# Another order for a planned kernel of attention, a rational MLP and a top-1 mixture of experts: new priority tables, some planner costs, the expert's choice marked as exclusive with GpSimd

## The chip, the cores and the metric

The kernel runs on one core of a Trainium2 chip. A core has a matrix engine (TensorE; PE in the profile, with its weight loads as PEld), a vector engine (VectorE, DVE), a scalar engine (ScalarE, ACT), a general engine (GpSimd, POOL) and a queue engine (SyncE, SP) that here issues the transfers. Each runs its own list of instructions in order and waits on semaphores for the others. The metric is the device time of one execution in microseconds (us); lower is better.

## What is computed

Three stages in a row, each on the output of the one before, all in fp32 accuracy:

```python
# attention: 4 batches, 8 heads, 1152 keys of 64; queries are averaged in pairs (576 a batch)
q_pool = q.reshape(B, H, S // 2, 2, D).mean(axis=3)
attn = softmax(q_pool @ k.transpose(0, 1, 3, 2) / sqrt(D))
x = (attn @ v).transpose(0, 2, 1, 3).reshape(2304, 512)
# MLP with a rational activation, 512 -> 2048 -> 512
h = x @ w_in
g = (a[0] + a[1]*h + a[2]*h**2 + a[3]*h**3) / (1 + abs(b[0])*abs(h) + abs(b[1])*h**2 + 1e-6)
x = g @ w_out
# mixture of 8 experts, one per token, 512 -> 1024 -> 512
e_idx = argmax(x @ w_gate, axis=1)
for e in range(8):
    mask = e_idx == e
    out[mask] = gate_w[mask] * sigmoid(x @ w_ogate)[mask, e] * (relu(x[mask] @ w1[e]) @ w2[e])
```

## The kernel before

**Numbers.** Every fp32 operand of a large product is split into a high and a low half-precision part (16 bits each), and a product is three matmuls: high by high, high by low, low by high. The splitting is elementwise work for DVE, ACT and POOL, and it is most of what these do.

**Attention** is cut into 144 units (`unit`, lines 894 to 1006): a tile of 128 queries of one head against all 1152 keys. A unit has two score products on PE (lines 925; 1024 keys into the PSUM tile `sab`, the last 128 into a small bank), the row maximum on DVE (the score reduction, line 935, over 1024 keys; line 938 for the rest), a one-column bias on DVE or ACT (lines 945 and 947), the exponentials on ACT (line 953), the split of the probabilities (the rounding copy `ph`, lines 962 and 964, and the residual `pl`, line 968: POOL or DVE), a transposing transfer by SP, and the product with v on PE (line 977). Before a batch, k, v and q are loaded, scaled and split; the scales are worked out in chains of tiny DVE operations (line 730), which write `small`.

**The MLP** is cut into 18 tiles of 128 tokens with four groups of 512 hidden columns each, 72 in all (`group`, lines 1257 to 1345): four first-layer blocks on PE (lines 1276 to 1278), some ten elementwise operations (lines 1287 to 1330: DVE's fused steps at line 1287, the numerator's products at line 1291 and fused steps at line 1315 on POOL or DVE, abs, logarithm and exponential on ACT), the split of the result, and the second-layer matmuls (lines 1338 to 1340). One buffer, `tw`, is shared by all groups. The last DVE row of a group at line 1287 reads `scr` and `hps` and writes `scr`.

**Routing** (`route`, lines 1397 to 1470): behind a tile's fourth group its output is evacuated with a scale (`yr`, line 1443, ACT or DVE), transposed on PE (line 1446), multiplied with the gates (line 1409); then comes the choice, a chain of four tiny DVE operations (`choose`, line 730; the last writes `oh`, 128x8), the ranks on PE (lines 1418 and 1419: by `tri` and by ones), the gate weights, and an indirect transfer by POOL (line 1465) that scatters the tokens to an array in DRAM sorted by expert (`ysort`).

**Experts.** After tile 9 the planned part picks the expert with most tokens so far, and loads and splits its weights; after tile 15 a row at line 1540 reads that expert's count, SP pads its rows, and five slots of 128 sorted rows each are worked (`first_slots`, first layer at lines 1609 to 1611, second at 1625 to 1627) while tiles 16 and 17 end. Then a table of the other slots is made and the rest runs in slots with a fixed order, which the planner doesn't touch.

**What sets the order.** Every operation of the planned part is handed to `plan.add` with a key (about the number of the unit beside which it is due), the engines that may do it with a cost each, what it reads and writes, and whether it is exclusive. `order` (lines 444 to 527) is a list scheduler: again and again it places, over all engines, the operation that can start first by its own account of times; equal starts go by key. To the key is added an entry of `SHIFT` for the operation's kind (name, engines, and a suffix: "." for keys under 9, ":" under 24, "!" from 128, none between), and for an operation that several engines may do, an entry of `BIAS` for kind and engine is added to the start. Exclusive (`port`) means that the planner doesn't place the operation on DVE or POOL while it believes the other of the two to be in another exclusive one; operations that may go to several engines are exclusive if nothing else is said. `plan.trace` then writes each engine's instructions in the order found. So the tables and costs set two things only: which engine does an operation, and where it stands in that engine's list.

```python
if ops[i][8] and e in other:
    s = max(s, port[other[e]])
```

Of the kernel before, what the change touches and what calls it, by code (L numbers as in the profile page):

```python
# [21 lines left out]
SHIFT = {'X/PE': -203.5,  # L22
 'X/PE!': -61.3,
 'X/PE.': 56.9,
 'X/PE:': -56,
 'bias/DVE+ACT': -115.7,
 'bias/DVE+ACT!': 88.3,
 'bias/DVE+ACT.': -79.5,
 'bias/DVE+ACT:': 1.9,
 'chain cf/DVE': 397.7,  # L30
 'chain cf/DVE.': -13.6,
 'chain den/DVE': 102,
 'chain den/DVE!': 66.3,
 'chain den/DVE.': -3.2,
 'chain esc/DVE': 181.5,
 'chain esc/DVE!': 33.5,
 'chain esc/DVE:': 86.2,
 'chain ps/DVE': 9.5,
 'chain ps/DVE!': -176.9,
 'chain ps/DVE:': 17.4,  # L40
 'chain qsc/DVE': -94,
 'chain qsc/DVE.': -4.7,
 'chain qsc/DVE:': -143.1,
 'chain ro/DVE': -47,
 'chain ro/DVE!': 78.8,
 'chain ro/DVE:': 0.2,
 'chain rt/DVE': -0.1,
 'chain rt/DVE!': 21.5,
 'chain rt/DVE:': 1.3,
 'chain sc/DVE': -76.9,  # L50
 'chain sc/DVE.': -188.4,
 'chain wsi/DVE.': 9.2,
 'chain wso/DVE.': -74.1,
 'chain xm/DVE': 15.3,
 'chain xm/DVE.': -1,
 'chain xs/DVE': 284.9,
 'chain xt/DVE': -4.1,
# [48 lines left out]
 'nBl/DVE+POOL.': 6,
 'nrm/DVE+ACT+POOL': 352.5,
 'nrm/DVE+ACT+POOL.': -4.5,
 'nrm/DVE+ACT.': -8.4,
 'nrmQ/DVE+ACT': 835.2,  # L110
 'nrmQ/DVE+ACT:': -0.2,
 'nrmQ/DVE:': -71.1,
 'nrmQl/DVE+POOL': -0.8,
 'nrmQl/DVE+POOL.': -15.4,
 'nrml/DVE+POOL': -3.4,
 'nrml/DVE+POOL.': 57.1,
 'oacc/POOL+DVE': -278.6,
 'oacc/POOL+DVE!': 4.6,
 'oacc/POOL+DVE:': -6.8,
 'p/ACT': 366.4,  # L120
 'p/ACT!': -10.2,
 'p/ACT.': 272.1,
 'p/ACT:': 120.4,
 'p/DVE.': -24,
 'pad/SP.': 10.6,
 'padded/SP!': -19,
 'pads/SP': 173.4,
 'pc/ACT': -66.9,
 'pc/ACT!': -102.5,
 'pc/ACT.': 1.3,  # L130
 'pc/ACT:': 0.8,
 'ph/DVE+ACT+POOL': 4.9,
 'ph/DVE+ACT+POOL!': 5.8,
 'ph/DVE+ACT+POOL.': -21.1,
 'ph/DVE+ACT+POOL:': -2.9,
 'ph/DVE:': 4.3,
 'pl/POOL+DVE': -790.8,
 'pl/POOL+DVE!': 41.7,
 'pl/POOL+DVE.': 7.4,
 'pl/POOL+DVE:': -76.9,  # L140
 'pt/SP': -17.5,
 'pt/SP!': 4.5,
 'pt/SP.': -3.8,
 'pt/SP:': 3,
 'pv/PE': -149.5,
 'pv/PE!': -47.1,
 'pv/PE.': 27.7,
 'pv/PE:': 4.4,
 'qT/SP': 42.7,
 'qT/SP.': 0.7,  # L150
 'qT/SP:': -35.1,
 'qm/DVE': 460.9,
 'qm/DVE.': 1.1,
 'qm/DVE:': 1.4,
 'qr/SP': 72.3,
 'qr/SP.': 170.6,
 'qr/SP:': -5.2,
 'qs/DVE+POOL': 19.6,
 'qs/DVE+POOL.': 107.8,
 'raw/SP.': -1.3,  # L160
 'rawz/SP!': 29.3,
 're/ACT': 188,
 're/ACT!': -29.6,
 're/ACT:': -103.1,
 'rs/ACT': 151.9,
 'rs/ACT!': -59.9,
 'rs/ACT:': -15.8,
 'run/DVE': 0.9,
 'run/DVE!': -22.7,
 'sab/PE': 16,  # L170
 'sab/PE!': 156.4,
 'sab/PE.': 20.1,
 'sab/PE:': -5.3,
 'scr/DVE.': 250.6,
 'sq/ACT.': -4.8,
 'sq/DVE:': -35.2,
 'sum/PE': 10.9,
# [382 lines left out]
def tile_attn_moe_moe2(  # L560
# [139 lines left out]
    xhf = acut(DM, F32, ["xhf0", "xhf1"])  # L700
# [1255 lines left out]
```

## Time and profile before

| what | value |
|---|---|
| times of three runs | 1224.31, 1235.28, 1235.61 us |
| median | 1235.28 us |
| the profiled execution, its own time | 1225.93 us |
| its span | 1224.2 us |
| its granted TensorE clock, mean | 0.937 |
| DVE busy | 971.0 us, 79% of the span |
| PE busy | 975.9 us, 80% |
| ACT busy | 800.7 us, 65% |
| POOL busy | 610.1 us, 50% |

The profile is of one execution, taken by the hardware profiler. Busy is the time in which an engine ran an instruction; a share over the whole span mixes stretches with different limits, so the stretches are read apart. Durations of rows include what an instruction waits inside its own execution. A row of the timeline has its start and length in us, the engine, the line, the operation, what it writes and reads with shapes, and in square brackets the idle time of the engine just before it with what ended that.

### The profile page before, as it was taken

How to read it: one execution, taken by the hardware profiler on the slowest of the kernel's cores; microseconds unless marked ns; L12 is line 12 of the kernel's file. 1: busy time of each engine (PE TensorE's matmuls, PEld its weight loads, DVE VectorE, ACT ScalarE, POOL GpSimd, SP SyncE). 2: the span in 40 equal slices, each digit the busy share in tenths (PEclk: the TensorE clock that was granted, in tenths of full speed). 3: DMA queues.
4: the chain of work that ended last, by engine and by line, in shares of the span. 5: the costliest groups of instructions: out<-in, count | busy, mean ns of one | idle time of the engine just before them, and what ended most of it. 6: DMA issues, size and time to landing. Idle time of an engine off the chain costs nothing. (4 is left out here: it accounts for less than half of the span.)

```text
span 1224.2 us, 30760 instructions
## 1 busy us (share of the span) xinstructions
PE 975.9 (80%) x12213; PEld 687.7 (56%) x12213; DVE 971.0 (79%) x2122; ACT 800.7 (65%) x1174; POOL 610.1 (50%) x421
## 2 busy tenths in 40 slices
PE   0245558878787798889898989898988799899986
PEld 0022345556554566656666765575656577577763
DVE  6998777798999898999998899989897864333354
ACT  1664749789786899799799868885775541122213
POOL 0023358657486786476587756766876530000000
PEclk9997569989899899999999999999999899999998
DMA  8889559989789989989989986798564502333351
GB/s 330 253 184 246 98 125 202 153 148 200 169 151 190 203 159 182 192 165 161 189 150 174 167 173 142 143 195 136 106 117 111 147 27 54 90 79 79 76 177 29
DMA packets 493058, 185.78 MB, mean 152 GB/s; under 512 B 454164, under 2 KB 472596, under 8 KB 492821
## 3 DMA queue, kind: packets, MB, share of 16 engines
q1 hardware_dynamic: 489933, 174.16, 70.9%
q0 software_dynamic: 2960, 9.46, 2.3%
q8 instruction: 99, 1.62, 0.5%
q14 instruction: 66, 0.54, 0.1%
HBM read 60.36 MB, written 11.82 MB: 59 GB/s over the span
## 5 line engine op out<-in xcount | busy, mean ns | idle before, releaser
L968 POOL TENSOR_TENSOR att<-att 128x1152 f16<-128x1152 f32 x91 | 221.8, 2439 | 187.3 <-ACT att L962 165.6
L1276 PE MATMUL hps<-scr,winh 128*128 128x128 f16 x1152 | 218.2, 227 | 25.9 <-DVE scr L1287 21.6
L1277 PE MATMUL hps<-scr,winh 128*128 128x128 f16 x1152 | 218.4, 227 | 0.0
L1278 PE MATMUL hps<-scr,winl 128*128 128x128 f16 x1152 | 218.3, 227 | 0.0
L977 PE MATMUL shared<-att 128*128 128x65 f16 (+3 forms) x4320 | 155.5, 201 | 59.4 <-DMA att<-att 41.6
L935 DVE TENSOR_REDUCE small<-sab 128x1 f32<-128x1024 f32 x144 | 175.0, 1216 | 23.5 <-PE sab L925 16.0
L977 PEld LDWEIGHTS <-att 128*128 128x128 f16 (+1 forms) x4320 | 144.3, 106 | 86.6 <-DMA att<-att 54.5
L953 ACT ACTIVATE att<-sab,small 128x1024 f32<-128x1024 f32 x144 | 172.8, 1200 | 18.4 <-DVE small L730 8.1
L1291 POOL TENSOR_TENSOR scr<-scr 128x512 f16<-128x512 f32 (+1 forms) x96 | 122.6, 1279 | 79.6 <-ACT scr L1330 33.5
L925 PE MATMUL sab<-att 128*128 128x512 f16 x512 | 145.1, 411 | 21.6 <-ACT att L953 13.4
L925 PEld LDWEIGHTS <-att 128*128 128x128 f16 x768 | 73.2, 103 | 122.9 <-issue 72.4
L1277 PEld LDWEIGHTS <-winh 128*128 128x128 f16 x1152 | 117.4, 102 | 43.5 <-issue 33.7
L1276 PEld LDWEIGHTS <-winh 128*128 128x128 f16 x1152 | 118.4, 103 | 16.4 <-issue 3.7
L1278 PEld LDWEIGHTS <-winl 128*128 128x128 f16 x1152 | 117.7, 102 | 0.0
L1287 DVE SCALAR_TENSOR_TENSOR scr<-scr,small,hps 128x512 f32<-128x512 f32 x144 | 106.5, 740 | 13.6 <-ACT hps L1326 7.2
L1609 PE MATMUL sab<-att 128*128 128x128 f16 x608 | 107.8, 223 | 7.6 <-DMA att<-att 5.2
L1338 PE MATMUL yps<-wouth,scr 128*128 128x512 f16 x288 | 109.9, 382 | 3.3 <-DVE small L730 2.3
L1340 PE MATMUL yps<-wouth,scr 128*128 128x512 f16 x288 | 110.1, 382 | 0.9 <-POOL scr L1291 0.9
L1339 PE MATMUL yps<-woutl,scr 128*128 128x512 f16 x288 | 110.1, 382 | 0.0
L1611 PE MATMUL sab<-att 128*128 128x128 f16 x608 | 107.7, 223 | 2.1 <-DVEq L1859 1.5
L1610 PE MATMUL sab<-att 128*128 128x128 f16 x608 | 107.8, 223 | 0.0
L962 ACT CAST att<-att 128x1152 f16<-128x1152 f32 x90 | 103.7, 1153 | 5.0 <-DMA att<-att 4.1
(226 smaller groups left out, 2351.8 us busy)
## 6 DMA issues: line engine op xcount, KB each, us to landing
att<-in_k_dram SPq DMA_DIRECT2D x16, 576.0 KB, 5.6
att<-in_q_dram SPq DMA_DIRECT2D x16, 512.0 KB, 4.6
att<-in_moe_w_dram SPq DMA_DIRECT2D x4, 2048.0 KB, 9.1
att<-in_v_dram SPq DMA_DIRECT2D x14, 576.0 KB, 4.6
woutl<-in_moe_w_out_dram SPq DMA_DIRECT2D x12, 512.0 KB, 7.6
att<-ysort SPq DMA_DIRECT2D x19, 257.0 KB, 3.0
att<-att SPq DMA_TRANSPOSE x137, 5.0
wouth<-in_moe_w_in_dram SPq DMA_DIRECT2D x4, 512.0 KB, 11.2
```

Of the source, the lines that this page charges most:

```text
L925: T.matmul(dst[:, d0:d0 + w], qT[:, H * x + 2 * i + t, :], rhs, start=(x == 0), stop=(x == 1))
L935: A(key - ahead - .6, {"DVE": 1.13}, lambda e: V.reduce_max(mm[:, 0, bi:bi + 1], ab, axis=AX.X), r=[f"sab{par}"] + mt, w=[f"mab{n}"] + ([f ...
L953: return lambda e: S.activation(dst, src, AF.Exp, bias=mm[:, 2, bi:bi + 1], scale=esc[:, 0, i:i + 1])
L968: lambda e: eng(e).tensor_tensor(out=phs[pb][:, 1], in0=p32, in1=ph(), op=SUB),
L977: T.matmul(pvb[p0:p0 + w, bi, 0:d], pt[:, lhs, p0:p0 + w], rhs[:, h, c, :], start=(c == 0 and lhs == 0 and rhs is vh), stop=(lhs == 2 * KC ...
L1276: T.matmul(hp, wh, xh[:, kc, :], start=(kc == 0), stop=False)
L1277: T.matmul(hp, wh, xl[:, kc, :], start=False, stop=False)
L1278: T.matmul(hp, wl, xh[:, kc, :], start=False, stop=(kc == KD - 1))
L1291: return lambda e: eng(e).tensor_tensor(out=out_, in0=i0, in1=i1, op=op)
L1338: T.matmul(yps, a, wouth[:, ff, :], start=(ff == 0), stop=False)
L1339: T.matmul(yps, a, woutl[:, ff, :], start=False, stop=False)
L1340: T.matmul(yps, b_, wouth[:, ff, :], start=False, stop=(ff == KF - 1))
```

## The change

The two tables are written anew with other numbers (237 and 136 entries before, 233 and 145 now), five of the planner's cost literals are set to measured lengths, and the choice of the expert is marked as exclusive. No operation is added, taken out or computed otherwise.

```diff
-SHIFT = {'X/PE': -203.5,
+SHIFT = {'X/PE': -189.5,
- 'pl/POOL+DVE': -790.8,
+ 'pl/POOL+DVE': -1071.9,
...
-BIAS = {('bias/DVE+ACT', 'ACT'): 63.85,
+BIAS = {('bias/DVE+ACT', 'DVE'): -0.87,
- ('ph/DVE+ACT+POOL', 'POOL'): 39.78,
+ ('ph/DVE+ACT+POOL', 'POOL'): 204.46,
...
-        A(key - ahead - 1.2, {"PE": 0.86 * f2}, smm(ab, [(0, 512), (512, 512)]), r=ins, w=[f"sab{par}"])
+        A(key - ahead - 1.2, {"PE": 0.9 * f2}, smm(ab, [(0, 512), (512, 512)]), r=ins, w=[f"sab{par}"])
...
-            A(key + .05 * jj, {"PE": 0.67}, g1(jj), r=[f"xT{s}"] + cols, w=[ht])
+            A(key + .05 * jj, {"PE": 0.7}, g1(jj), r=[f"xT{s}"] + cols, w=[ht])
...
-        LP = {"POOL": 0.68, "ACT": 0.62, "DVE": 0.33}
+        LP = {"POOL": 0.68, "ACT": 0.7, "DVE": 0.45}
...
-        A(k2 + .05, {"POOL": 1.9, "DVE": 0.65}, next_, r=[f"tq{tb}", c], w=[f"tp{tb}"])
+        A(k2 + .05, {"POOL": 2.0, "DVE": 0.65}, next_, r=[f"tq{tb}", c], w=[f"tp{tb}"])
...
-        A(key, {"ACT": 0.57, "DVE": 0.6},
+        A(key, {"ACT": 0.57, "DVE": 0.67},
           lambda e: S.activation(yr[:, 0:DM], yps, AF.Copy, scale=cf("iy")) if e == "ACT" else
...
-        chain(key + .08, choose, r=["y"], w=[f"rt{o}"])
+        chain(key + .08, choose, r=["y"], w=[f"rt{o}"], port=1)
```

The tables are five lines longer, so line 717 of the kernel before is line 722 of the changed one, and so on. What the tables do is seen in the order of the instructions. Three places follow; in all of them a row is line, operation, what it writes and reads, and the shape.

**DVE, the last score reduction of attention.** `sab` is the PSUM tile of the scores, `hps` that of an MLP group's first layer. Before, from row 1557 of DVE's list:

```order
L935 TENSOR_REDUCE small<-sab_75 128x1
L730 CAST small<-small 128x1
L1287 SCALAR_TENSOR_TENSOR scr<-scr,small,hps_77 128x512
L730 SCALAR_TENSOR_TENSOR small<-shared,small 128x4
L947 TENSOR_SCALAR small<-small 128x1
L730 RECIPROCAL small<-small 128x4
L1006 TENSOR_TENSOR att<-shared,small 128x256
L730 RECIPROCAL yr<-small 128x1
L748 SCALAR_TENSOR_TENSOR att<-att,small 128x1024 x2
L1315 SCALAR_TENSOR_TENSOR scr<-scr,small 128x512
L1291 TENSOR_TENSOR scr<-scr 128x512
L1287 SCALAR_TENSOR_TENSOR hps_77<-scr,small,hps_77 128x512
```

In the changed kernel the same reduction is row 1487:

```order
L940 TENSOR_REDUCE small<-sab_75 128x1
L735 TENSOR_SCALAR oh_89<-small 128x8
L1320 SCALAR_TENSOR_TENSOR scr<-scr,small 128x512
L735 SCALAR_TENSOR_TENSOR small<-shared,small 128x4
L735 SCALAR_TENSOR_TENSOR small<-yps,oh_89 128x8 x2
L735 RECIPROCAL small<-small 128x4
L735 CAST small<-small 128x1
L1292 SCALAR_TENSOR_TENSOR scr<-scr,small,hps_78 128x512
L1011 TENSOR_TENSOR att<-shared,small 128x256
L1292 SCALAR_TENSOR_TENSOR hps_78<-scr,small,hps_78 128x512
L943 TENSOR_SCALAR small<-shared,small 128x128
L1292 SCALAR_TENSOR_TENSOR scr<-scr,hps_78 128x512
```

The reduction moved 70 rows forward. Three more of the 72 MLP groups then end behind it.

**DVE, the first read of sorted rows.** Line 717 (now 722) takes the maximum of the first rows fetched from the sorted array; `att` is the storage that they lie in, and the rows at line 1287 (now 1292) are MLP steps. Before, from row 1623:

```order
L1287 SCALAR_TENSOR_TENSOR scr<-scr,hps_78 128x512
L717 TENSOR_REDUCE small<-att 128x1
L1555 TENSOR_SCALAR small<-small 128x1
L1556 TENSOR_SCALAR small<-small 128x1
L1557 TENSOR_SCALAR small<-small 128x1
L1287 SCALAR_TENSOR_TENSOR scr<-scr,small,hps_77 128x512
L717 TENSOR_REDUCE small<-att 128x1
L748 SCALAR_TENSOR_TENSOR att<-att,small 128x512
L1555 TENSOR_SCALAR small<-small 128x1
L1556 TENSOR_SCALAR small<-small 128x1
L1557 TENSOR_SCALAR small<-small 128x1
L1287 SCALAR_TENSOR_TENSOR scr<-scr,small,hps_77 128x512
```

Here the read stands right behind the last step of a group, and row 1639, five rows behind this piece, is tile 16's evacuation (line 1443). In the changed kernel:

```order
L1292 SCALAR_TENSOR_TENSOR hps_78<-scr,small,hps_78 128x512
L1292 SCALAR_TENSOR_TENSOR scr<-scr,hps_78 128x512
L1307 TENSOR_SCALAR scr<-scr,small 128x512
L1296 TENSOR_TENSOR scr<-scr 128x512
L1292 SCALAR_TENSOR_TENSOR scr<-scr,small,hps_77 128x512
L1320 SCALAR_TENSOR_TENSOR scr<-scr,small 128x512
L722 TENSOR_REDUCE small<-att 128x1
L1560 TENSOR_SCALAR small<-small 128x1
L1561 TENSOR_SCALAR small<-small 128x1
L1562 TENSOR_SCALAR small<-small 128x1
L1292 SCALAR_TENSOR_TENSOR scr<-scr,small,hps_77 128x512
L1623 TENSOR_SCALAR small<-att,small 128x1
```

Four MLP rows (lines 1307, 1296, 1292, 1320) now stand between that last step and the read, and tile 16's evacuation isn't in DVE's list: ACT does it, as it does those of tiles 15 and 17.

**PE, the ranks of the last tile.** They are the two products by `tri` and by ones; `sab` is here the output of an expert's first layer (line 1609 to 1611), and `shared` that of its second. Before:

```order
L1610 LDWEIGHTS att
L1610 MATMUL sab_74<-att 128x128
L1611 LDWEIGHTS att
L1611 MATMUL sab_74<-att 128x128
L1418 LDWEIGHTS tri
L1418 MATMUL yps<-oh_89,tri 128x8
L1419 LDWEIGHTS ones_82
L1419 MATMUL yps<-oh_90,ones_82 128x8
L1609 LDWEIGHTS att
L1609 MATMUL sab_75<-att 128x128
L1610 LDWEIGHTS att
L1610 MATMUL sab_75<-att 128x128
```

In the changed kernel:

```order
L1632 LDWEIGHTS att
L1632 MATMUL shared<-att 128x512
L1633 LDWEIGHTS att
L1633 MATMUL shared<-att 128x512
L1634 LDWEIGHTS att
L1634 MATMUL shared<-att 128x512
L1423 LDWEIGHTS tri
L1423 MATMUL yps<-oh_89,tri 128x8
L1424 LDWEIGHTS ones_82
L1424 MATMUL yps<-oh_90,ones_82 128x8
L1614 LDWEIGHTS att
L1614 MATMUL sab_74<-att 128x128
```

The ranks now stand within the first layer of another slot, one earlier, with more of the first slots' blocks behind them: 20 of the first layer and 31 of the second, where 17 and 24 stood.

## Rows read from the trace of the kernel before

**Rows 1.** The page's parts 1 and 2: busy time of each engine; DVE in 40 slices.

```profile
PE 975.9 (80%) x12213; PEld 687.7 (56%) x12213; DVE 971.0 (79%) x2122; ACT 800.7 (65%) x1174; POOL 610.1 (50%) x421
DVE  6998777798999898999998899989897864333354
```

**Rows 2.** Windows: stretch, length, busy PE PEld DVE ACT POOL, clock, DMA share, GB/s.

```profile
92.00:214.00 122.00, 73.98 (x906) 49.74 (x906) 97.80 (x180) 82.06 (x112) 63.32 (x39) 0.72 0.82 168
214.00:857.00 643.00, 555.05 (x7567) 393.76 (x7566) 588.75 (x1362) 534.90 (x801) 425.79 (x272) 0.95 0.91 169
914.50:951.60 37.10, 30.78 (x376) 23.99 (x374) 29.71 (x55) 21.47 (x38) 23.14 (x20) 0.91 0.49 116
951.60:1046.00 94.40, 85.44 (x897) 61.82 (x896) 56.20 (x148) 34.36 (x58) 27.99 (x27) 0.96 0.26 73
1046.00:1224.20 178.20, 157.43 (x1704) 112.02 (x1703) 67.17 (x127) 42.72 (x51) 16.88 (x18) 0.97 0.34 87
```

**Rows 3.** Timeline of DVE, 914 to 1023 us, single rows.

```profile
914.54 1.23 DVE L935 TENSOR_REDUCE small<-sab 128x1 f32<-128x1024 f32 x1 [0.56 <-PE sab L925]
...
922.67 0.68 DVE L1287 SCALAR_TENSOR_TENSOR scr<-scr,hps 128x512 f32<-128x512 f32 x1
...
946.93 0.16 DVE L730 TENSOR_REDUCE small<-yps 128x1 f32<-128x8 f32 x1
...
951.62 0.16 DVE L1540 SCALAR_TENSOR_TENSOR small<-small 128x8 f32<-128x8 f32 x1
...
963.87 0.69 DVE L1287 SCALAR_TENSOR_TENSOR scr<-scr,hps 128x512 f32<-128x512 f32 x1
...
986.77 0.17 DVE L730 TENSOR_REDUCE small<-yps 128x1 f32<-128x8 f32 x1 [2.11 <-PE yps L1409]
```

**Rows 4.** Timeline of DVE and PE at the first read of sorted rows.

```profile
969.90 0.69 DVE L717 TENSOR_REDUCE small<-att 128x1 f32<-128x512 f32 x1 [5.34 <-DMA att<-ysort]
...
976.45 1.12 PE L1446 MATMUL yps<-ident,yr 128*128 128x128 f32 x4 [6.40 <-DVE yr L1443]
```

**Rows 5.** Timeline of PE, 1046 to 1063 us, the rows with a wait.

```profile
1046.58 0.38 PE L1627 MATMUL shared<-att 128*128 128x512 f16 x1 [0.78 <-ACT att L1639]
...
1054.15 0.23 PE L1609 MATMUL sab<-att 128*128 128x128 f16 x1 [2.24 <-DVE small L1557]
...
1062.35 0.22 PE L1609 MATMUL sab<-att 128*128 128x128 f16 x1 [2.67 <-DMA att<-att]
```

**Rows 6.** Tiny chains: timeline at 605 us, then line 730's forms (min/median/max ns), one group's mean.

```profile
604.98 2.36 DVE L730 TENSOR_SCALAR oh<-small 128x8 bf16<-128x8 f32 x1
...
604.94 2.37 POOL L968 TENSOR_TENSOR att<-att 128x1152 f16<-128x1152 f32 x1
...
L730 DVE TENSOR_SCALAR oh<-small x18: 217/404/2364, 233.7 to 1022.9; 128x8 bf16<-128x8 f32 x18
...
L730 DVE SCALAR_TENSOR_TENSOR small<-small x54: 137/212/2406, 44.2 to 1024.3; 128x1 f32<-128x1 f32 x18, 128x2 f32<-128x2 f32 x16, 128x8 f32<-128x8 f32 x16, 128x4 f32<-128x4 f32 x4
...
L730 DVE SCALAR_TENSOR_TENSOR small<-small 128x8 f32<-128x8 f32 x16 | 9.6, 616 | 0.0
```

**Rows 7.** Instructions by line and form: busy us, mean ns, idle before, releaser.

```profile
L730 DVE TENSOR_SCALAR oh<-small 128x8 bf16<-128x8 f32 x18 | 13.6, 753 | 0.2
L947 DVE TENSOR_SCALAR small<-small 128x1 f32<-128x1 f32 x115 | 23.7, 206 | 0.7
L968 DVE TENSOR_TENSOR att<-att 128x1152 f16<-128x1152 f32 x9 | 14.3, 1594 | 0.0
L968 DVE TENSOR_TENSOR scr<-att,scr 128x1152 f16<-128x1152 f32 x7 | 9.6, 1374 | 0.2 <-ACT scr L962 0.2
L1291 DVE TENSOR_TENSOR scr<-scr 128x512 f32<-128x512 f32 x41 | 30.4, 744 | 0.7 <-ACT scr L1300 0.7
L1315 DVE SCALAR_TENSOR_TENSOR scr<-scr,small 128x512 f32<-128x512 f32 x33 | 28.9, 878 | 0.1
L968 POOL TENSOR_TENSOR att<-att 128x1152 f16<-128x1152 f32 x91 | 221.8, 2439 | 187.3 <-ACT att L962 165.6 <-issue 14.2 <-DVE att L964 3.4
```

More of the change, by code (lines that the diff above doesn't have):

```diff
@@ L360 @@
- ('wih/ACT+DVE.', 'DVE'): 66.77,
- ('wil/POOL+DVE.', 'POOL'): 62.66,
- ('woh/ACT+DVE.', 'ACT'): -0.68,
- ('woh/ACT+DVE.', 'DVE'): 9.87,
- ('wol/POOL+DVE.', 'POOL'): 3.57,
+ ('pl/POOL+DVE!', 'POOL'): -1,
+ ('pl/POOL+DVE.', 'DVE'): 88.35,
+ ('pl/POOL+DVE.', 'POOL'): 2.03,
+ ('pl/POOL+DVE:', 'DVE'): 88.28,
+ ('pl/POOL+DVE:', 'POOL'): -0.16,
+ ('qs/DVE+POOL', 'DVE'): 0.04,
+ ('qs/DVE+POOL', 'POOL'): 32.87,
+ ('qs/DVE+POOL.', 'DVE'): 59.25,
+ ('qs/DVE+POOL.', 'POOL'): -1,
+ ('qs/DVE+POOL:', 'DVE'): 0.79,
@@ new lines @@
+ ('tp/POOL+ACT+DVE', 'POOL'): 1.04,
+ ('tp/POOL+ACT+DVE!', 'ACT'): 15.57,
+ ('tp/POOL+ACT+DVE!', 'DVE'): 0.12,
+ ('tp/POOL+ACT+DVE!', 'POOL'): 0.32,
+ ('tp/POOL+ACT+DVE:', 'ACT'): 9.89,
+ ('tp/POOL+ACT+DVE:', 'DVE'): 52.34,
+ ('tp/POOL+ACT+DVE:', 'POOL'): 9.81,
+ ('tp/POOL+DVE!', 'DVE'): -0.32,
+ ('tp/POOL+DVE!', 'POOL'): 69.52,
+ ('tp/POOL+DVE:', 'DVE'): -0.11,
+ ('tq/ACT+DVE!', 'ACT'): 0.24,
+ ('tq/ACT+DVE!', 'DVE'): 14.61,
+ ('tq/ACT+DVE:', 'ACT'): 88.21,
+ ('tq/ACT+DVE:', 'DVE'): -1,
+ ('tw/POOL+ACT+DVE', 'ACT'): 0.41,
@@ new lines @@
+ ('tw/POOL+ACT+DVE', 'DVE'): 0.55,
+ ('tw/POOL+ACT+DVE', 'POOL'): 76.1,
+ ('tw/POOL+ACT+DVE!', 'ACT'): 0.06,
+ ('tw/POOL+ACT+DVE!', 'DVE'): 0.94,
+ ('tw/POOL+ACT+DVE!', 'POOL'): 16.2,
+ ('tw/POOL+ACT+DVE:', 'ACT'): -0.99,
+ ('tw/POOL+ACT+DVE:', 'DVE'): 8.01,
+ ('tw/POOL+ACT+DVE:', 'POOL'): -0.12,
+ ('vh/DVE+ACT+POOL', 'ACT'): -1,
+ ('vh/DVE+ACT+POOL', 'DVE'): 18.82,
+ ('vh/DVE+ACT+POOL.', 'DVE'): 16.5,
+ ('vh/DVE+ACT+POOL.', 'POOL'): 36.44,
+ ('vl/DVE+POOL', 'DVE'): -1,
+ ('vl/DVE+POOL', 'POOL'): 3,
@@ L370 @@
+ ('xh/DVE+ACT+POOL!', 'ACT'): -1,
+ ('xh/DVE+ACT+POOL!', 'DVE'): 7.97,
+ ('xh/DVE+ACT+POOL!', 'POOL'): -1,
  ('xh/DVE+ACT+POOL.', 'ACT'): -1,
[L371 to L381 removed]
@@ L382 @@
[L382 to L394 removed]
+ ('xh/DVE+ACT+POOL.', 'DVE'): 4.14,
+ ('xh/DVE+ACT+POOL.', 'POOL'): -1,
+ ('xh/DVE+ACT+POOL:', 'DVE'): 5.88,
@@ new lines @@
+ ('xl/POOL+DVE', 'DVE'): -0.26,
+ ('xl/POOL+DVE', 'POOL'): 47.77,
+ ('xl/POOL+DVE!', 'DVE'): -0.96,
+ ('xl/POOL+DVE!', 'POOL'): 40.52,
+ ('xl/POOL+DVE.', 'POOL'): 12.74,
+ ('xl/POOL+DVE:', 'DVE'): -0.63,
+ ('xl/POOL+DVE:', 'POOL'): 1.38,
+ ('yT/DVE+ACT', 'ACT'): -1,
+ ('yT/DVE+ACT', 'DVE'): -0.41,
+ ('yT/DVE+ACT!', 'ACT'): 9.92,
+ ('yT/DVE+ACT!', 'DVE'): -1,
+ ('yT/DVE+ACT:', 'ACT'): -0.96,
+ ('yT/DVE+ACT:', 'DVE'): 27.89,
+ ('yr/ACT+DVE', 'ACT'): 0.79,
+ ('yr/ACT+DVE', 'DVE'): 1.08,
+ ('yr/ACT+DVE!', 'ACT'): -1,
@@ L397 @@
+ ('yr/ACT+DVE:', 'ACT'): 2.79,
+ ('yr/ACT+DVE:', 'DVE'): 23.91,
+ ('zh/ACT+DVE!', 'ACT'): -1,
+ ('zh/ACT+DVE!', 'DVE'): -0.84,
+ ('zl/DVE+POOL!', 'DVE'): -0.15,
+ ('zl/DVE+POOL!', 'POOL'): 2.71,
+ ('zxh/ACT+DVE!', 'ACT'): 0.12,
+ ('zxh/ACT+DVE!', 'DVE'): 0.73}
 class Plan:
```

656 lines of the change are left out of this document (299 added, 357 removed).

## The prediction, made before the changed kernel was run

> **What bounds the kernel now.** I read the page's busy times and its slices first, then the busy time of each engine in stretches, then single rows where stretches meet. DVE is busy 971.0 us of 1224.2 and PE 975.9 [rows 1], which looks like a tie; it isn't one, because the two are busy in different places. The slices show DVE at 9 or nearly so up to about slice 30 and at 3 to 6 behind it. In the main stretch, 214 to 857 us, DVE is busy 588.75 of 643.00 us (92%), PE 86%, ACT 83%, POOL 66%; in the one ahead of it DVE idles 24.2 us of 122.00 [rows 2]. Up to about 915 us DVE is the engine that everything waits for, with 24.2 + 54.3 = 78.5 us idle in these two. Attention ends at 914.54, where the last score reduction stands; what is left up to 951.6 is rational activation (MLP) with DVE at 80% and the granted clock at 0.91 [rows 2, 3]. From there PE carries the end: 85.44 of 94.40 us, and 157.43 of 178.20 us in the expert slots, whose code is not in the planned order and stands as it was [rows 2].
>
> So an edit of the order can pay in three ways: fewer us of work on DVE ahead of 915, fewer waits between 915 and 1063 where the stages meet, or fewer stalls between DVE and POOL.
>
> **The change, part by part.** No instruction is added or taken away; PE and SP issue as many as before. The literals for costs alter only where the planner believes an engine free, so they act through the order and have no price of their own.
>
> *Engine choice.* Comparing the two orders kind by kind and pricing each by its own row: DVE gives up 28 of the one-column biases (28 x 0.206 = -5.8) and 9 of 16 residuals of the probabilities (9 x 23.9/16 = -13.4), and takes 9 products (9 x 0.744 = +6.7) and 9 fused steps of the numerator (9 x 0.878 = +7.9) [rows 7]. The kinds left, small ones, add some 4. That is about -0.7 us: DVE has the same work. ACT takes the 28 biases and 11 more rounding copies; POOL has 28 instructions fewer. Both have room (POOL is at 50% and ACT 65% of the span), so I price this at 0.
>
> *Attention ends sooner, MLP later.* The last score reduction of attention is row 1487 of DVE's order and was 1557. Pricing every DVE row ahead of it by its kind gives 893.5 us where it was 921.0 (records overlap a little at their ends, so a sum can exceed the time that passed): -27.6. But three more MLP groups are left then (13 of 72 unfinished on DVE, before 10). Group ends follow one another at 8.24 us in that stretch (five periods from 922.67 to 963.87, the rows of line 1287 [rows 3]), so they cost 3 x 8.24 = +24.7. What remains is -2.9; counting instead all DVE work ahead of the row that reads the first expert's count (951.62, [rows 3]) gives -1.2. I take **-1**, with bounds -4 and +4.
>
> *The wait for sorted rows.* At 969.90 DVE has idled 5.34 us for the rows fetched from the sorted array. The evacuation of tile 16 (line 1443) is queued on DVE behind that wait, and PE's transposes wait for it 6.40 us [rows 4]. In the new order four MLP rows of DVE stand ahead of the row that waits, 0.7 to 0.9 us each (some 3 us), PE has five more first-layer blocks of the first slots there, and the evacuation is ACT's. If the fetch is as late as before, DVE idles some 3 us less: **-3**. Bounds: 0 (ACT waits there as well, for the scale worked out from the same rows) and -6.4 (all of it).
>
> *The end of the planned part.* After the ranks of the last tile PE has 20 first-layer and 31 second-layer blocks of the first slots where it had 17 and 24: 3 x 12 + 7 x 3 = 57 matmuls more. At the 85.44 us for 897 matmuls of 951.6 to 1046 [rows 2] they are 5.4 us of work that covers the table's making and the first fetch of the static slots. The waits there are 0.78 + 2.24 + 2.67 = 5.7 us [rows 5]. I take **-4**, bounds 0 (the slots start from something later in the chain) and -5.7.
>
> *The mark on the choice.* The choice of the expert is a chain of four tiny DVE rows; the last, of 128x8, takes 217 ns at best and 753 on average, 18 times [rows 6, 7]. One of 2.36 us lies exactly beside a POOL residual of 2.37 [rows 6]: it waits for POOL inside its own time. All 18 cost 18 x (0.753 - 0.217) = 9.7 us too much. The mark makes the planner place them where it believes POOL idle. What such a mark is worth is seen in the scale chains, marked already: their 128x8 row still averages 616 ns where the shortest of its kind takes 137, an excess of 479 beside 536 [rows 6]. A mark so far takes one ninth: **-1**, bounds 0 and -9.7.
>
> The Trainium skill ("SBUF — State Buffer", section "Who interferes with whom") says that whichever of the two engines issues first holds the shared pair for its whole instruction and the other is blocked fully, and that issue order decides, not the shape. The trace agrees by the 2.36 beside 2.37 us. By that rule a mark in a plan helps only where the real times follow the plan's, and the term would be 0 instead of -1.
>
> *Waits redrawn.* Every other edge is drawn anew through thousands of rows. In single places cover is thinner (units with under 13 us of PE work between the second score product and the product with v: 27, before 20), in others thicker. I find no sign for the sum and put 0, with bounds of +15 and -15, a fifth of DVE's 78.5 us of idle time.
>
> **Sum:** -1 - 3 - 4 - 1 = -9 on the profiled execution's 1225.93, so 1217. That execution lies 9.35 below the median of 1235.28, two of three runs being near 1235 and one at 1224; by the median the sum gives 1226. A new median can come from either level. I predict **1222**.
>
> **Rivals.**
>
> *No net effect.* Stalls and waits only change places: DVE's work is the same to 0.7 us, PE's is the same, the mark is worth nothing. For it speaks that four fifths of DVE's time is unchanged row for row in kind; against it that the two waits near 970 and 1050 lie where PE is the bound and get cover. 1226 to 1240, middle 1231.
>
> *POOL's relief pays.* POOL's lists are shorter and, late, hold residuals (2.44 us each [rows 7]) but hardly the copies ahead of them. If half of the stalls in the two 128x8 rows vanish (9.7 + 16 x 0.479 = 17.4, so -8.7), and a tenth of DVE's idle time in 92 to 857 (-7.9), less the 1 counted above, the sum is -9 - 15.6 = -25: 1201 to 1210, middle 1205. Against it: ACT has 34 instructions more, and where the residuals wait it is for ACT (165.6 of their 187.3 us [rows 7]).
>
> The skill ("Perfetto Trace Analysis", "Optimizing Scalar/DVE Operations") says that moving work between GpSimd and DVE might not help while moving it to Scalar may when DVE is saturated. By that the move to ACT would lie nearer this rival; no run so far shows it.
>
> *Slower: the MLP stretch is longer.* 13 groups instead of 10 are left when attention's matmuls have ended, and each group there hangs on one work buffer and a chain that goes between DVE and ACT. Tile 16's choice came 39.8 us after tile 15's (946.93 to 986.77 [rows 3]), 10.0 us a group; the clock was 0.91 in the stretch ahead [rows 2]. The break-even is at 8.24 + 9/13 = 8.9 us a group. At 10.0 the sum is 13 x 1.76 - 9 = +14: 1240 on the profiled execution, 1249 on the median; with redrawn waits on top up to 1260. Against it: the 39.8 us hold the 6.4 us wait that should shrink.
>
> **How the numbers follow.** My forecast (a gain of 5 to 16, 1210 to 1232) has 0.42, no net effect 0.20, relief 0.16, the longer MLP stretch 0.22. The range, 1198 to 1250, holds the forecast, no net effect, nearly all of relief and some two thirds of the slower case, with the bounds of the redrawn waits; the forecast's own range is 1210 to 1232. One per cent, about what a measurement of this kernel tells from no change, is 1222.9 and 1247.6. Faster: all of relief and two thirds of the forecast, 0.44. Slower: most of the slower case, 0.16. Same: 0.40.
>
> **What would show it.** Right: the last score reduction near 887 instead of 914.54, the row of the first count within 4 us of 951.62, DVE's idle before the first read of sorted rows near 2 instead of 5.34, PE's 6.40 halved, the three waits near 1050 together under 2 us, the 128x8 choice at 600 to 750 ns on average. Wrong: group ends more than 8.9 us apart after attention has ended (slower rival); DVE busy well over 92% in the main stretch (relief); or the new last score reduction no sooner than 905, since then the waits inside attention have grown and the sum has no first term.

## The result, and the profile after

The change made the kernel slower: 1246.52 us (median of 18 runs) against 1228.53 (median of 18), a ratio of 1.0129 with a 95% interval of 1.0111 to 1.0148. The first three of these 18 gave the 1235.28 that the forecast started from. I had forecast 1222, with the largest share of the chances, 0.44, on faster: the sum was -9 and the change +18. The time lies inside the range of 1198 to 1250, but on the other side of no change.

The page of the changed kernel, parts 1 and 2 (its lines of code are five further down: 717 is now 722, 935 is 940):

```profile
PE 980.4 (79%) x12213; PEld 689.7 (55%) x12213; DVE 960.7 (77%) x2099; ACT 817.4 (66%) x1208; POOL 576.0 (46%) x393
DVE  6998787788898878999778899898989773233354
```

Against [rows 1]: DVE is busy 10 us less, POOL 34 less, ACT 17 more, and the span of this one execution is 22.4 us longer (1246.6; the medians differ by 18.0). No engine is busier by as much as the span is longer (PE has 4.5 us more), so the time was not added as work, it was added as waiting. Where, the windows show (stretch, length, busy PE, PEld, DVE, ACT, POOL, clock, DMA share, GB/s), of the changed kernel, the last two cut at its own marks, the end of attention and the read of the first count:

```profile
92.00:214.00 122.00, 75.24 (x982) 50.75 (x982) 97.25 (x183) 82.08 (x111) 65.24 (x38) 0.71 0.86 175
214.00:857.00 643.00, 538.35 (x7294) 380.79 (x7293) 560.02 (x1298) 534.24 (x801) 412.58 (x263) 0.95 0.91 167
913.40:974.50 61.10, 52.59 (x596) 39.23 (x594) 52.35 (x104) 35.94 (x67) 24.74 (x24) 0.91 0.42 87
974.50:1246.60 272.10, 245.53 (x2642) 175.60 (x2639) 119.71 (x270) 76.43 (x110) 35.13 (x38) 0.97 0.31 81
```

and of the kernel before, the stretch that answers to the last:

```profile
951.60:1224.20 272.60, 242.87 (x2601) 173.84 (x2599) 123.37 (x274) 77.08 (x108) 44.87 (x45) 0.97 0.31 82
```

The marks, from the changed kernel's DVE timeline (start, length, then the row; in brackets the idle time ahead and its releaser). The rows of line 1292 are the ends of the first, second and seventh MLP group behind attention's end, and the last one of the thirteenth, the last of all:

```profile
913.41 1.21 DVE L940 TENSOR_REDUCE small<-sab 128x1 f32<-128x1024 f32 x1
...
918.37 0.67 DVE L1292 SCALAR_TENSOR_TENSOR scr<-scr,hps 128x512 f32<-128x512 f32 x1
...
930.04 0.69 DVE L1292 SCALAR_TENSOR_TENSOR scr<-scr,hps 128x512 f32<-128x512 f32 x1
...
973.21 0.69 DVE L1292 SCALAR_TENSOR_TENSOR scr<-scr,hps 128x512 f32<-128x512 f32 x1
...
974.52 0.16 DVE L1545 SCALAR_TENSOR_TENSOR small<-small 128x8 f32<-128x8 f32 x1
...
993.44 0.69 DVE L722 TENSOR_REDUCE small<-att 128x1 f32<-128x512 f32 x1 [3.40 <-DMA att<-ysort]
...
1018.23 0.69 DVE L1292 SCALAR_TENSOR_TENSOR scr<-scr,hps 128x512 f32<-128x512 f32 x1
```

With [rows 2, 3] the 22.4 us split in three. Attention ends, that is, its last score reduction starts, at 913.41, before 914.54: -1.1. From there to the first count it takes 61.1 us, before 37.1: +24.0. The rest takes 272.1, before 272.6: -0.5. So attention used up nearly all the DVE time that the new order spares it: in the main stretch DVE is busy 560.02 of 643 us (87%) where it was 588.75 (92%). The DMA engines' share there is 0.91 in both kernels.

DVE's waits from 92 to 857 us (what waited, for whom: us in all, times, longest), those of 5 us and more, in the changed kernel:

```profile
DVE small L940 <- PE sab L930: 21.3, 26, 2.1
DVE small L943 <- PE shared L982: 19.0, 16, 3.5
DVE scr L1292 <- ACT hps L1331: 9.0, 10, 2.3
DVE scr L1322 <- PE hps L1283: 7.1, 5, 1.7
DVE small L735 <- PE shared L649: 5.1, 4, 2.2
DVE small L735 <- PE shared L982: 5.0, 5, 2.1
```

and in the kernel before:

```profile
DVE small L935 <- PE sab L925: 13.4, 20, 2.2
DVE small L938 <- PE shared L977: 7.9, 11, 1.4
DVE small L938 <- PE shared L925: 7.3, 12, 2.0
DVE scr L1317 <- PE hps L1278: 6.0, 7, 3.0
DVE small L935 <- PE sab L922: 5.3, 3, 4.3
DVE scr L1287 <- ACT hps L1326: 5.2, 10, 1.2
```

Four of them stand in both lists, and each of the four is longer on average (the first 0.82 us a time where it was 0.67, the second 1.19 where it was 0.72), two of them also more frequent; no single wait is above 4.3 us. Idle time in this stretch rose from 78.5 to 107.7 us; summed over the view, waits for PE went from 51 to 68 and for ACT from 12 to 24. No single stall carries the loss. By an estimate that prices each DVE row of the two orders by its kind and compares with the starts in the traces, the changed kernel has fallen behind by nothing at unit 36, by some 15 us at unit 72 and by some 28 at unit 108, and roughly holds there.

### The profile page after: what moved, and what is told of

Same layout as the page of the kernel before. It is cut to its first block, busy times and chain, and to the rows that moved or that the text cites. A ratio compares the mean times of both kernels' runs of the same rounds, so it can differ in the third digit from the quotient of the medians.

```text
span 1246.6 us, 30811 instructions
## 1 busy us (share of the span) xinstructions
PE 980.4 (79%) x12213; PEld 689.7 (55%) x12213; DVE 960.7 (77%) x2099; ACT 817.4 (66%) x1208; POOL 576.0 (46%) x393
## 5 line engine op out<-in xcount | busy, mean ns | idle before, releaser
L973 POOL TENSOR_TENSOR att<-att 128x1152 f16<-128x1152 f32 x95 | 229.5, 2416 | 147.5 <-ACT att L967 119.5
L940 DVE TENSOR_REDUCE small<-sab 128x1 f32<-128x1024 f32 x144 | 175.1, 1216 | 32.9 <-PE sab L930 21.6
L1296 POOL TENSOR_TENSOR scr<-scr 128x512 f16<-128x512 f32 (+1 forms) x87 | 110.9, 1277 | 109.6 <-ACT scr L1335 61.3
L973 POOL TENSOR_TENSOR scr<-att,scr 128x1152 f16<-128x1152 f32 x42 | 101.3, 2412 | 42.1 <-ACT scr L967 32.3
L967 ACT CAST att<-att 128x1152 f16<-128x1152 f32 x97 | 111.8, 1152 | 12.1 <-DMA att<-att 11.3
L1343 PE MATMUL yps<-wouth,scr 128*128 128x512 f16 x288 | 111.9, 389 | 2.7 <-DVE small L735 2.1
L1345 PE MATMUL yps<-wouth,scr 128*128 128x512 f16 x288 | 111.8, 388 | 0.0
L1614 PE MATMUL sab<-att 128*128 128x128 f16 x608 | 106.0, 221 | 5.8 <-ACTq L1864 3.4
L1616 PE MATMUL sab<-att 128*128 128x128 f16 x608 | 106.0, 221 | 3.5 <-DVEq L1864 2.6
```

The source lines that it names most:

```text
L940: A(key - ahead - .6, {"DVE": 1.13}, lambda e: V.reduce_max(mm[:, 0, bi:bi + 1], ab, axis=AX.X), r=[f"sab{par}"] + mt, w=[f"mab{n}"] + ([f ...
L967: S.copy(ph(), p32)
L973: lambda e: eng(e).tensor_tensor(out=phs[pb][:, 1], in0=p32, in1=ph(), op=SUB),
L1343: T.matmul(yps, a, wouth[:, ff, :], start=(ff == 0), stop=False)
L1345: T.matmul(yps, b_, wouth[:, ff, :], start=False, stop=(ff == KF - 1))
```

## The experiments

"Before" is the kernel before, run beside each; a difference in us is between medians unless a row of the profile is named. The theories: **P** or **D**, one resource sets attention's pace (the transposing queue, or DVE); **E**, **M** or **L**, one part of the change does the harm (engines, mark, lengths); **W** or **N**, in-order lists in which each engine waits for the others, so that the loss has no one place. The letters A, Q, R and S belong to single expectations and are explained there.

**Fixed sequences, e1 to e4.** The planner's result is replaced by a list of operation and engine that is written into the kernel:

```diff
-        for _, i, e in self.order():
+        for i, e in ORDER:
             self.ops[i][2](e)
```

> The operations stand in the sequence of the kernel before, but each goes to the engine that the changed kernel gives it (28 biases and 11 rounding copies more on ACT, POOL with fewer). Theory P (pace): attention goes at a pace that DVE does not set alone, so the sequence, which leaves MLP work behind, makes the loss: 1225 to 1233 us, no slower than before. Theory E (engines): the longer way through ACT in every unit makes the loss: 1240 to 1248. Theory W (waits drawn anew by many small moves): something between, 1232 to 1242.

> The sequence of the changed kernel with the engines of the kernel before. Theory P: 1242 to 1250 us, as slow as the changed kernel. Theory E: 1225 to 1234, the loss is gone. Theory W: between.

> Kernel before, same engines, one thing moved: from attention's unit 36 to 108 the MLP's operations slide back to 280 places later in the sequence, so that 27 us less of DVE work stands ahead of the last score reduction, as in the changed kernel; behind it they slide forward again. Theory P: attention cannot use the room, its last score reduction comes at 905 to 916 us and the MLP's rest is paid behind it: 1240 to 1250. Theory W: the reduction comes at 885 to 895, and the total stays at 1222 to 1234.

> Changed kernel, same engines, the reverse: the MLP's operations slide up to 200 places forward from unit 36 on, so that 16 of the 27 us of DVE work stand ahead of the last score reduction again. Theory P: the reduction hardly moves (910 to 918 us), and the total falls by 8 to 14, to 1232 to 1239. Theory W: the reduction comes later by about 16 (927 to 932) and the total stays at 1243 to 1252.

Measured: 1309.92, 1342.16, 1370.07 and 1428.11 us beside 1232.32, that is 6.4% to 16.1% slower, with attention's end at 954 to 962 us in all four. All expectations missed, by far, and so the four don't tell P from E. What they show is that a sequence with the other kernel's engines, or with the MLP's operations moved by a few hundred places, is much slower than either kernel. In e1 DVE has the changed kernel's instructions, and its busy time is (page, part 1):

```profile
PE 997.1 (76%) x12213; PEld 699.3 (54%) x12213; DVE 1022.7 (78%) x2099; ACT 820.9 (63%) x1208; POOL 579.1 (44%) x393
```

1022.7 us for the 2099 instructions that take 960.7 in the changed kernel: 62 us more inside DVE's own instructions. The traces show where. Call a DVE row long if it takes over 0.25 us more than the short rows of its kind (the tenth percentile, for kinds of three rows and more); what the long rows take beyond the short ones adds up to 54.2 us in the kernel before, 43.9 in the changed one and 100.1 in e1, and every one of them (48, 41 and 85 rows) overlaps an instruction of POOL, where only some 53 to 59% of the other rows do. So these are stalls of the kind seen in [rows 6]. That they come because operations no longer stand where the planner kept DVE and POOL apart is likely, but not shown by itself. The same count says that the 10 us by which the changed kernel's DVE is less busy are fewer stalls and not less work. I used finer cuts from here on.

**One part of the change alone, e5, e6, e10, e11.** The planner draws a new order each time.

```diff
-        chain(key + .08, choose, r=["y"], w=[f"rt{o}"])          # e5: before plus this line
+        chain(key + .08, choose, r=["y"], w=[f"rt{o}"], port=1)  # e6: changed kernel without it
-        A(key, {"ACT": 0.57, "DVE": 0.6},                        # e11: before plus this literal
+        A(key, {"ACT": 0.57, "DVE": 0.67},                       # e10: before plus all five
```

> Kernel before with one part of the change alone: the choice of the expert is marked as exclusive; tables and costs as before, so the planner draws a new order from the same tables. Theory M (the mark is worth its stalls): the 128x8 choice falls from 753 to under 400 ns on average and the time to 1218 to 1226 us. Theory W (tables fit one order; any other draw from them loses cover): the choice falls as well, and the time rises to 1235 to 1255.

> Changed kernel without the mark; tables and costs of the change. If the mark does the harm: 1226 to 1234 us with the choice at 650 to 800 ns. Theory W: its tables no longer fit the order either, 1245 to 1265.

> Kernel before with the five cost literals of the change alone, tables as before. Theory W: a new draw from tables that fitted another one, 1240 to 1275 us, as with the mark alone. Theory L (better lengths make a better order): 1218 to 1228.

> Kernel before with one literal alone: the evacuation of a tile's output costs DVE 0.67 instead of 0.6, an operation done 8 times by DVE. By itself nothing to gain or lose. If the loss comes from what a literal says: within 3 us of the kernel before. Theory W: any change of the draw costs, 1235 to 1270 us.

| run | us | before | ratio |
|---|---|---|---|
| e5, mark alone | 1273.80 | 1225.54 | 1.0391 (1.0330 to 1.0453) |
| e6, change without mark | 1259.86 | 1225.54 | 1.0253 (1.0190 to 1.0316) |
| e10, five costs alone | 1290.02 | 1227.21 | 1.0520 (1.0473 to 1.0567) |
| e11, one cost alone | 1260.96 | 1227.21 | 1.0269 (1.0242 to 1.0296) |

One literal, raised by 0.07 for an operation that DVE does eight times, costs 34 us. With the change itself that makes five draws, and all are slower, by 18, 34, 34, 48 and 63 us. Theories M and L fall for the mark and the costs: no part helps or harms by what it says. The mark does what it says to the choice (359 ns on average in e5 with it, 632 in e6 without it, 753 before) and the time rises all the same. A reading that fits is that the tables of before suit the order that they draw with exactly these costs, and that another draw loses cover; how the tables were made is not shown here, and five draws are few. The change brings tables of its own and loses least.

**One kind of operation, e9 and e12.** e9 fixes the changed order and gives the biases back to the engines of before; e12 keeps the order of before and writes the last step of the choice in the accumulating form:

```diff
-            V.tensor_scalar(oh, sc, bs, None, op0=ALU.is_equal)
+            V.tensor_scalar(oh, sc, bs, 0.0, op0=ALU.is_equal, op1=ALU.add, accum_out=ps)
```

> Order of the changed kernel, fixed; only the one-column bias of each unit goes to the engine that the kernel before gave it (36 of 144 differ, most of them from ACT back to DVE, each at its place in the sequence). Theory E (the way through ACT lengthens each unit's chain: 383 ns and a hop instead of 206 ns on the engine that made the maximum): 1232 to 1241 us and the last score reduction 5 to 12 us sooner. Theory W (the loss lies in no kind of operation): within 5 us of the changed kernel's 1246.5.

> Kernel before, its order untouched; the last operation of the choice is written in the form that also sums its output (the form of line 938, which shows no stall in 144 rows), so that it need not wait for POOL. Its mean should fall from 753 to under 330 ns. If DVE's stalls are worth their length where DVE is the bound: 1219 to 1224 us, 5 to 9 less. If DVE then only waits for something else: 1226 to 1231.

e9: 1256.03 us, ratio to before 1.0219 (1.0192 to 1.0246), where the changed kernel has 1.0129, and attention ends at 921.99, later than in the changed kernel. Both expectations missed (E by 15 us, W by 5): the biases' way through ACT is not shown to cost anything, but after e1 a fixed sequence with other engines is not a clean test of theory E. e12: ratio 0.9992 (0.9963 to 1.0022). Its choice, by line and form (busy us, mean ns, idle before), then that of the changed kernel, whose choice is marked and in the plain form:

```profile
L730 DVE TENSOR_SCALAR_CACHE_REDUCE oh<-small 128x8 bf16<-128x8 f32 x18 | 3.9, 217 | 0.2
L730 DVE DVE_READ_ACCUMULATOR oh<-small 128x1 f32 x18 | 1.5, 82 | 0.0
...
L735 DVE TENSOR_SCALAR oh<-small 128x8 bf16<-128x8 f32 x18 | 6.0, 334 | 0.1
```

The stalls of [rows 7] are gone in e12, 13.6 us are now 3.9 (and 1.5 for reading the accumulator), and the kernel is as fast as before: of some 8 us spared on DVE at most 4.5 can have reached the time, by the interval, and the median shows none. DVE is busy 92% around them, and yet attention ended at 918.08 in this run's profile, 3.5 us later than before.

**The transposing transfer, e7 and e8.**

```diff
-        A(key + .3, {"SP": 2.65}, lambda e: SP.dma_start_transpose(out=pt, in_=phs[pb].rearrange("p o l -> p (o l)")),
+        A(key + .3, {"SP": 2.65}, lambda e: (G.memset(pt[:, 0:8], 0.0) if n < 2 else None, SP.dma_start_transpose(out=pt[:, 8:], in_=phs[pb].rearrange("p o l -> p (o l)")[:, 1024:])),
```

> Order of the kernel before, fixed. The transposing transfer of the probabilities moves 10 of its 18 blocks of 128 columns (the first 8 are left at zero, so eight blocks of keys lack their high parts; values and routing change, the work on every engine does not). It is there to be compared with the next one. Theory P (the transposing queue sets attention's pace, 92.5% busy from 286 to 692 us): the last score reduction comes at 885 to 905 us instead of 914.5, as DVE, 92% busy, soon takes over. Theory W: 905 to 915.

> The same shortened transfer with the order of the changed kernel, fixed. Theory P: with the queue out of the way the 27 us less of DVE work ahead of it show, the last score reduction comes 18 to 28 us ahead of the run before, and the total lies within 8 us of it. Theory W: the waits are between engines and stay, the reduction comes within 8 us of the run before, the total 14 to 24 above it.

The routing differs, so totals compare only with each other: 1340.79 and 1362.41, a difference of 21.6. The last score reductions, of e7:

```profile
882.71 1.23 DVE L935 TENSOR_REDUCE small<-sab 128x1 f32<-128x1024 f32 x1
```

and of e8 (a fixed order written into the kernel before, so with its line numbers):

```profile
883.26 1.21 DVE L935 TENSOR_REDUCE small<-sab 128x1 f32<-128x1024 f32 x1
```

The main stretch in e7, then in e8 (columns as above):

```profile
214.00:857.00 643.00, 568.04 (x7873) 405.85 (x7872) 609.48 (x1409) 551.87 (x835) 449.57 (x291) 0.97 0.66 125
214.00:857.00 643.00, 557.71 (x7687) 397.44 (x7686) 588.91 (x1353) 557.55 (x842) 428.19 (x272) 0.96 0.67 126
```

The transfer matters: the DMA engines' share falls from 0.91 to 0.66 and 0.67, and attention ends 32 and 30 us sooner. But P's second half fails: with the queue relieved, DVE's spared work still doesn't show, and the two orders end attention within 1 us of each other again.

**What sets attention's pace, e13 to e15, e17, e18.** Each shortens one engine's part in every unit (e17 and e18: from unit 17 on), with the order of before (e14: the changed one) untouched. The pieces are cut out of longer lines, marked by three dots:

```diff
-... V.reduce_max(mm[:, 0, bi:bi + 1], ab, axis=AX.X)             # e13, e14
+... V.reduce_max(mm[:, 0, bi:bi + 1], ab[:, 0:512], axis=AX.X)
-                    for x in range(2):                           # e15, start and stop at each
+                    for x in range(1):
-                S.copy(ph(), p32)                                # e17, hw = 576 from unit 17
+                S.copy(ph()[:, 0:hw], p32[:, 0:hw])
-... eng(e).tensor_tensor(out=phs[pb][:, 1], in0=p32, in1=ph(), op=SUB)                       # e18
+... eng(e).tensor_tensor(out=phs[pb][:, 1, 0:hw], in0=p32[:, 0:hw], in1=ph()[:, 0:hw], op=SUB)
```

> Kernel before, order untouched; the score reduction (line 935, 144 times 1.22 us) looks at 512 of its 1024 columns, so the maximum that is subtracted misses some keys, which the softmax bears. DVE has some 75 us less to do ahead of the last reduction. Theory D (DVE, 92% busy, sets attention's pace): the last reduction comes 55 to 75 us sooner, at 840 to 860. Theory N (each engine waits in its order for the others, and DVE's time is only one link): 10 to 35 us sooner, 880 to 905, DVE's busy share falls to 82 to 87%.

> The same in the changed kernel. Theory D: 855 or sooner. Theory N: 10 to 35 us sooner than 913.4, and the total stays 10 to 25 us above the run with the order of before.

> Kernel before, order untouched; the score products take the high part of the queries alone, so PE spares half of 0.86 us in each of 144 units, some 60 us. Theory D: the last reduction moves by under 10 us. Theory N: 10 to 35 us sooner, as PE is a link of the chain as well (51 of DVE's 79 us of waits are for it).

> Kernel before, order untouched; from unit 17 on ACT's rounding copy of the probabilities takes 576 of 1152 columns (the other half keeps what an earlier unit left there, and the residual makes up for it). ACT is spared some 110 times 0.5 = 55 us ahead of the last score reduction. Theory A (ACT, 83% busy, sets the pace, and its 17 us more in the changed order ate what DVE was spared): the last reduction 25 to 50 us sooner, 865 to 890. Theory Q (the transposing queue sets it): a shorter way to the queue does not make the queue faster: under 10 us sooner, 905 to 914.

> Kernel before, order untouched; from unit 17 on the residual of the probabilities (POOL 2.44 us, 112 or so of the 127 units) is worked out for 576 of 1152 columns (the other half keeps an earlier unit's). POOL is spared some 135 us. Theory Q: under 10 us sooner. Theory R (POOL's residual is the long link before each transfer): 20 to 45 us sooner, 870 to 895.

The page of e13, part 1, and the last score reduction from its DVE timeline, then from e14's:

```profile
PE 974.5 (80%) x12213; PEld 686.4 (56%) x12213; DVE 909.2 (74%) x2122; ACT 799.3 (65%) x1174; POOL 609.6 (50%) x421
```

```profile
910.74 0.69 DVE L935 TENSOR_REDUCE small<-sab 128x1 f32<-128x512 f32 x1
...
903.30 0.68 DVE L940 TENSOR_REDUCE small<-sab 128x1 f32<-128x512 f32 x1
```

In e13 DVE is busy 61.8 us less than in [rows 1] (the reductions alone take 76.5 less), and attention ends 3.8 us sooner. The kernel takes 1223.86 us beside 1229.33 (0.9944, 0.9920 to 0.9969). In e14 DVE is busy 51 us less than in the changed kernel (909.5 for 960.7), and attention ends 10.1 us sooner. Theory D wanted 55 or more in both: it falls by these two runs. DVE's busy time, 92% of the stretch, does not set its pace one for one. Theory N's 10 to 35 us missed in e13 and came, at their edge, in e14. Of e15, e17 and e18 the last score reductions are at

```profile
899.46 1.22 DVE L935 TENSOR_REDUCE small<-sab 128x1 f32<-128x1024 f32 x1
```

```profile
942.87 1.23 DVE L935 TENSOR_REDUCE small<-sab 128x1 f32<-128x1024 f32 x1
```

```profile
890.24 1.22 DVE L935 TENSOR_REDUCE small<-sab 128x1 f32<-128x1024 f32 x1 [0.56 <-PE sab L925]
```

Each end of attention is from one profile; e12 ended it 3.5 us later than before in the same order, so e13's 3.8 can't be told from none.

| shortened | busy time spared, us (page) | attention's end against 914.54 | total, ratio |
|---|---|---|---|
| e13, DVE | 61.8 | -3.8 | 0.9944 |
| e15, PE | 56.4 | -15.1 | 0.9898 |
| e18, POOL | 126.0 | -24.3 | 0.9812 |
| e7, transposing transfer | 10 of 18 blocks moved | -31.8 | not comparable |
| e17, ACT | 49.3 | +28.3 | 1.0211 |

e15, e17 and e18 have two runs each. e15 fits theory N. e18 fits theory R and speaks against Q, by which a shorter way to the queue moves the end by under 10 us. e17 went against both of its theories. Its page, then e18's:

```profile
PE 980.9 (78%) x12213; PEld 689.0 (55%) x12213; DVE 994.8 (79%) x2122; ACT 751.4 (60%) x1174; POOL 612.8 (49%) x421
...
PE 967.8 (81%) x12213; PEld 681.0 (57%) x12213; DVE 934.3 (78%) x2122; ACT 799.3 (67%) x1174; POOL 484.1 (40%) x421
```

In e17 ACT does 49 us less, and DVE's unchanged instructions take 24 us more than in [rows 1]. By the count of long rows used for e1, their excess went from 54.2 to 80.2 us, and again each of them lies beside an instruction of POOL: the 24 us are such stalls. That they come because residuals on POOL now start earlier is likely; the run doesn't prove it, nor that the stalls are the whole of the 28 us. e18, which shortens the residuals, has DVE at 934.3 us, 37 less than before, with the same instructions: 11 in 16 residuals of its own, shortened too, and most of the rest in the long rows, whose excess is 27.8. e14's total is 1238.37 us, 14.5 above e13, so the gap between the two orders stays when DVE has 50 to 60 us to spare in either.

**Both orders in one kernel, e16**, another list in the place of `ORDER`.

> The order of the kernel before up to unit 72's reduction (492 us), the changed order behind it; at that place the two have the same DVE work behind them to 4 us. By the two traces the changed order had lost 15 of its 27 us up to there. Theory A (the loss is spread along the order): half of it, 1234 to 1243. Theory S (one place ahead of unit 72, from which the rest follows): 1225 to 1232.

1241.24 us beside 1229.33 (1.0104, 1.0026 to 1.0182; two runs only). Its last score reduction:

```profile
905.03 1.22 DVE L935 TENSOR_REDUCE small<-sab 128x1 f32<-128x1024 f32 x1
```

With half of the changed order the loss is about 12 us, by the interval 3 to 22, which is theory A's range, but doesn't tell it from the whole 18. Attention ends 9.5 us sooner than before, where the changed order ends it 1.1 sooner. So some of what attention lost is back without the changed order's first half, which speaks for a loss that is spread along the order and not for one place ahead of unit 72. I didn't run the reverse joint.

**What is left behind attention.** From attention's end to the first count it takes 37.1 us before and 35.6 to 37.4 in the six other runs with the order of before (e7, e12, e13, e15, e17, e18, the rows of lines 935 and 1540): ten groups are left in each. It takes 61.1 us in the changed kernel and 59.8 to 61.4 in e8, e9, e14 and e16: thirteen are left. Three groups more cost 22 to 26 us in every run, wherever attention ends; what differs between the runs of one order is when it ends.

No version here beats both kernels; those that are faster leave out part of the computation.

## Why the prediction was wrong, by its own steps

**The premise.** "Up to about 915 us DVE is the engine that everything waits for" is the step that failed. I read it from the busy share alone, 92%. By e13 and e14 it is wrong: 62 us less of DVE's busy time bring attention's end 3.8 us forward in one order, 51 us less bring it 10.1 forward in the other. The trace hinted at it: 51 of DVE's 78.5 us of idle time are for PE, so DVE is waited for and waits in turn, and in the same row of [rows 2] the DMA engines' share is 0.91.

**Attention ends sooner, MLP later.** The term was -27.6 + 24.7, cut to -1. The second half was right: three more groups were left, and the stretch took 24.0 us more. The first half is the term that the premise spoilt: it priced every microsecond of DVE work taken out ahead of attention's end as a microsecond of time, and it measured -1.1 instead of -27.6. These two together, +22.9, are the whole result of 22.4. I had named the sign by which to see it ("no sooner than 905, since then the waits inside attention have grown"), and gave the case no chance and no price: the full price of that failure, +24.7, stood in the sum.

**Waits redrawn.** I put 0 with bounds of 15 on either side. Five draws gave totals of +18 to +63. In hindsight there was a case for a sign: if the order of before is the best of many, another draw loses on average, and the term isn't symmetric about nothing. The 29 us by which DVE's idle time grew from 92 to 857 us are this term, nearly twice its bound: it is the loss in the first half above, seen from the side of the waits.

**The wait for sorted rows.** Right in what happens: DVE idles 3.40 us there instead of 5.34, the evacuation is ACT's, and PE's 6.40 us are gone: the transposes follow it without a wait. It was worth less than that: near it PE now waits 3.5 us, once, for DVE's line 1292, where before such waits came to 0.7 in all behind the first count. ACT's row and PE's:

```profile
998.92 0.69 ACT L1447 ACTIVATE yr<-yps,small 128x512 f32<-128x512 f32 x1 [0.76 <-PE yps L1345]
```

```profile
1001.24 0.62 PE L1451 MATMUL yps<-ident,yr 128*128 128x128 f32 x4
```

**The end of the planned part.** Forecast -4, and under 2 us of waits near 1050. PE's waits from 1036 to 1110 us in the changed kernel:

```profile
PE sab L1614 <- ACTq L1864: 3.4, 2, 2.2
PE sab L1616 <- DVEq L1864: 1.2, 1, 1.2
PE shared L1632 <- ACT att L1644: 0.8, 1, 0.8
```

That is 5.4 us beside the 5.7 of [rows 5]; the waits for the table went, and waits of the first static slots (line 1864) came in their place. Together with the step before, 7 us were forecast for the stretch behind the first count and 0.5 came (272.6 to 272.1): PE's idle time there fell from 29.7 to 26.6, and 2.7 us of PE's work moved in from ahead of it.

**The mark.** It did more to the stalls than I thought (the choice averages 334 ns; forecast 600 to 750), and no gain from it shows: e12 takes all of them away without one. Its bound of -9.7 priced an instruction's length in full on an engine whose time did not set the pace.

**Engine choice.** 0 was right as far as work goes. Its price can't be told from that of the order: in e9 giving one kind back in a fixed order made the kernel some 10 us slower still.

**The rivals.** The slower one had the time close (1240 to 1249), by another mechanism: groups more than 8.9 us apart. The first seven group ends are 9.1 apart ((973.21 - 918.37)/6), all thirteen 8.3 ((1018.23 - 918.37)/12), so its sign showed only at first; and the stretch of 61.1 us for seven is 8.7 a group, where 37.1 for four was 9.3. The groups were not slower, there were more of them and they began no sooner. That the time fell within this rival's range is luck. Of relief by POOL the first half came, as DVE's stalls beside POOL fell by 10 us, but not the time: its second half, less idle time of DVE, turned into 29 us more.

**Left open.** What sets attention's pace, and so why its waits grew. The transposing transfer, the residuals and the score products each move its end when shortened, DVE's reductions little, ACT's copies the wrong way. The DMA engines, busy 0.91 in both orders, are a candidate for a common link, and e7 and e8 show that their load matters; but e15 and e18 move the end with the transfers as they were, and a busy share is no proof here either. That both orders end attention at the same time (914.54 and 913.41, 882.71 and 883.26) while one has 27 us less of DVE's work may also be chance: with the shorter reduction the changed order ends it 7.4 us sooner (910.74 and 903.30).

## What to carry to other kernels

A busy share of 92% is no proof that an engine sets the pace: shorten its work in place and look, before you price a microsecond of it as a microsecond of the kernel. Where five engines run fixed lists against each other, price what is left behind (three groups, 24 us) in full and what is taken out in front at nothing until a run shows otherwise. And give a redrawn order a price of its own: here all five redraws cost time, and one literal out of five did 2.7%.

## What the runs showed of the hardware that I had not expected

A 128x8 comparison on DVE that takes 217 to 2364 ns in its plain form, the longest beside a residual on POOL, takes 208 to 223 ns in each of 18 cases in the form that also accumulates (e12), though an instruction of POOL ran beside 12 of them. And less work on one engine can go with longer instructions on another: with ACT's rounding copies halved, DVE's same 2122 instructions took 994.8 us instead of 971.0, and every DVE row over 0.25 us longer than the short ones of its kind lay beside one of POOL (e17).
